# A chunk-selecting attention with a layer-norm MLP on one core: the hand-written order of all steps laid out anew, with 24 fewer products on zeros

## The chip, the core and the metric

The kernel runs on one core of a Trainium2 chip. A core has five engines that run side by side, each its own list of instructions in order: TensorE (PE: products; its weight loads are shown as PEld), VectorE (DVE), ScalarE (ACT), GpSimd (POOL) and SyncE (SP), which here only asks for transfers. Transfers (DMA) are asked for from SP, ACT and POOL. SBUF is the memory that the engines work from, PSUM the small memory that PE writes its results to. The metric is the device time of one execution in microseconds (us); the median of three runs is given.

## What is computed

Two stages, both in one kernel; shapes are batch 4, 8 heads, sequence 768, head width 64, and a model width of 512 with a hidden width of 2048.

```python
k_min, k_max = min and max of k over chunks of 32 positions      # 24 chunks
ub = sum_d max(q * k_min, q * k_max), later chunks masked         # bound of each query on each chunk
top_chunks = argsort(ub)[..., -6:]
scores = q k^T / 8, kept where the key's chunk is chosen and key <= query
x = softmax(scores) v, heads side by side                         # 4 x 768 x 512
xn = (x - mean) / sqrt(var + 1e-6) * g_ln
out = x + max(xn @ w_ch1, 0) @ w_ch2
```

## The kernel before

**Tiles and stages.** A sequence is six tiles of 128 positions. A *group* g (0 to 15) is a pair of heads of a batch: g = 4 * batch + pair. The groups of batch 0 (0 to 3) are loaded and prepared tile by tile for all heads at once (steps with a name ending in t: ldt, turnt, kboundt, and so on); the first tile of every batch has its own steps (names ending in a: lda, turna, smma, sexpa, diaga, valuesa, norma; the number is the batch); the groups 4 to 15 are prepared one by one (ldb, turn, kbound, ...). The MLP works on *units* u of two or three tiles: units 0 and 1 are the first tiles of the batches, unit 2 + 2b holds tiles 1 and 2 of batch b, unit 3 + 2b its tiles 3 to 5.

**Steps.** Each step is a small function; its parts go to one engine, or to two or three.

| what | steps | engine, lines |
|---|---|---|
| loads of q and k | ldt.tile.kn/qn, lda.batch.kn/qn, ldb.group.kn/qn | SP, the lda of q ACT; L233, L206, L216 |
| loads of v, W1 and W2 in quarters | ldvt, ldva, ldv; w1.j; w2.j | POOL; L242, L209, L226; L190; L199 |
| q and k turned, so that the head width lies on the partitions | turnt, turna; turn | PE into PSUM, L254, L355; DVE, L427 |
| k bounds of a tile | kboundt, kbounda; kbound | DVE, L259/260, L360/361; L460/461 |
| k copied into the ring of keys | kcopyt, kcopya, kcopy | ACT, L122 (a helper's line) |
| bounds laid out for the product | kdiagt, kdiag | POOL, L270 to L279; L471 to L477 |
| q high part, low part, positive parts | qhit, qlot, qrelt, qringt | ACT L288; DVE L291, L297/298, L122 |
| bound products, mask, mask turned, mask into the ring | boundst, lowst, selectt, masktt, mringt | PE L311; ACT L122; DVE L327 to L332; PE L340; DVE L122 |
| scores, exponential, causal edge | smm/smma, sexp/sexpa, diag/diaga | PE L563, L381; ACT L574, L388; POOL L582, L395 |
| times v, divided | values/valuesa, norm/norma | PE L598, L406; DVE L612, L415 |
| layer norm | pstat/pstata, centre, rstd | DVE L649, L421; L659; DVE and POOL L667, L670 |
| normalized x turned | xtp and xtc (units 0, 1, 2), xt (others) | PE L683 and ACT L122; a transposing DMA from SP, L676 |
| W1 times the gain g_ln, by quarters | w1g.j | DVE L196 |
| first and second product of the MLP | m1.unit.m, relu, m2.unit.tile.j | PE L701; ACT L717; PE L730 |
| result, store | fin | DVE L739; SP L744 |
| mask rows, constants | rows, rows0, rrows.i; ident, idh, masks, caus, small, ones | POOL L134 to L139, POOL L183/184, DVE L122; POOL and DVE |

m1.u.m needs the W1 quarter m // 4, which w1g must have scaled; m2.u.i.j needs W2's quarter j and the relus of hidden part j.

**Products on zeros.** A step written with `@n`, where it runs on PE, is preceded by n products of 128x256 on a tile of zeros, into the PSUM tile that the step is about to write (`busy`, L116). Their result is overwritten. They keep PE busy while it has nothing to do. Before the first real step `warm.14` does fourteen of them.

**What sets the order.** The string ORDER lists all 956 steps. The loop behind it calls them one after the other and chains every instruction to the one before it on the same engine, so each engine's list, and SP's, ACT's and POOL's lists of transfers, have exactly this order:

```python
for ins in done[n:]:
    if ins.engine in queues:
        if ins.engine in ahead:
            tc.add_manual_dep(ins, ahead[ins.engine], inorder, reason="order")
        ahead[ins.engine] = ins.name
```

Waits between engines are put in by the framework from what each instruction reads and writes. It also makes two engines that read the same PSUM tile do so in the order of the list: a kcopyt that stands behind the kboundt of the same tile waits for it, and the other way round.

**Buffers.** PSUM is two pools: four small tiles (ps_t: turned tiles, bounds, masks, times-v of groups, second MLP product) and two large ones (ps_m: scores, first MLP product, times-v of first tiles). Loaded q and k tiles of 128x768 or less share six buffers (ldp), so the n-th load waits for the turn of the load six before it.

Of the kernel before, what the change touches and what calls it, by code (L numbers as in the profile page):

```python
# [19 lines left out]
def kernel(  # L20
# [714 lines left out]
    def fin(u, i, e=None):  # L735
# [147 lines left out]
```

## Time and profile before

| | us |
|---|---|
| median of 3 runs (283.73 to 283.98) | 283.79 |
| the profiled execution, its own time | 283.73 |
| its span, first to last instruction | 282.0 |
| PE busy | 265.9 |
| DVE busy | 208.5 |
| ACT busy | 181.4 |
| POOL busy | 110.2 |
| bytes moved | 31.01 MB |

The profile is one execution. Its parts read here: busy tenths of each engine in 40 slices; busy time by stretch; the timeline of one engine (start, length, line, output, input, idle before and what released it); the chain of work that ended last, followed back from the end; transfers with the time from request to landing. Busy times of PE overlap a little at their ends, which are modelled, so lengths of PE work are taken from start to start.

PE's first real product starts at 4.19 us, the unbroken stretch of MLP products at 41.80 us, and the last product ends at 278.8 us; DVE has most of its work done at 205 us, after which PE still has about 75 us of products.

### The profile page before, as it was taken

To read this page: it belongs to the slowest core of one execution; us is meant where nothing else is said; L and a number is where in the kernel's file an instruction comes from. 1 tells how busy PE (TensorE), PEld (TensorE's weight loads), DVE (VectorE), ACT (ScalarE), POOL (GpSimd) and SP (SyncE) were. 2 spreads that over 40 slices of the span, in tenths; PEclk is the share of its full clock that TensorE was granted. 3 is DMA by queue.
4 is the path that set the end of the run, shared out by engine and by line. 5 is a ranking of instruction groups with operands and counts; after the bars stand their busy time and mean duration, and the time that the engine had idled before them with its cause. 6 is when DMAs were issued, how large, how long until landed. Compare 5 with 4: busy or idle time off the path is not lost.

```text
span 282.0 us, 7100 instructions
## 1 busy us (share of the span) xinstructions
PE 265.9 (94%) x2785; PEld 188.2 (67%) x2785; DVE 208.5 (74%) x604; ACT 181.4 (64%) x241; POOL 110.2 (39%) x209
## 2 busy tenths in 40 slices
PE   8775889899999999899999999989999999999995
PEld 5654779687677666666786676669666665765552
DVE  5978999936999999899999999998835162501111
ACT  2365786643799896878779778886686575222420
POOL 8883847070524407958162252645230121100000
PEclk9999999999999999999999999999999999999999
DMA  8999999999368979997595769358140102021102
GB/s 164 209 207 187 138 154 142 190 135 116 25 120 175 188 107 140 123 149 108 97 125 128 124 162 136 53 86 76 30 127 2 40 37 74 19 42 74 74 9 105
DMA packets 126897, 31.01 MB, mean 110 GB/s; under 512 B 118032, under 2 KB 123920, under 8 KB 126864
## 3 DMA queue, kind: packets, MB, share of 16 engines
q1 hardware_dynamic: 92848, 22.16, 40.5%
q0 software_dynamic: 29328, 7.34, 27.8%
q10 hardware_dynamic: 4688, 1.05, 2.5%
q8 instruction: 22, 0.36, 0.6%
q14 instruction: 11, 0.09, 0.1%
HBM read 27.27 MB, written 6.29 MB: 119 GB/s over the span
## 4 chain that ended last, share of the span: by engine, by line
PE 75%; DVE 12%; POOL 4%; ACT 3%; issue 2%; SPq 2%; DMA 1%; DVEq 0%; POOLq 0%; ACTq 0%
PE mm L701 28%; PE yp L730 25%; PE mm L563 10%; PE sm L598 5%; PE ub L484 3%; DMA knb<-in_k_dram 1%; SPq L216 1%; PE trh L514 1%; ACT KB L122 1%; DVE bst L649 1%; DVE KA L122 1%; DVE KB L122 1%; POOL bdt L273 1%; ACT KA L122 1%; DVE kcs L260 1%
## 5 line engine op out<-in xcount | busy, mean ns | idle before, releaser
L574 ACT ACTIVATE pt<-mm 128x1024 f16<-128x1024 f32 (+2 forms) x96 | 81.9, 881 | 23.5 <-PE mm L563 22.2
L730 PE MATMUL yp<-w2b,hT 128*128 128x512 f16 (+2 forms) x400 | 93.6, 370 | 0.2 <-DVE x L612 0.2
L701 PE MATMUL mm<-xT,w1b 128*128 128x256 f16 (+1 forms) x640 | 89.5, 294 | 1.4 <-ACT hT L717 1.3
L717 ACT ACTIVATE hT<-mm 128x768 f16<-128x768 f32 (+1 forms) x56 | 50.2, 901 | 42.0 <-PE mm L701 38.5
L701 PEld LDWEIGHTS <-w1b 128*128 128x128 f16 x640 | 61.5, 98 | 22.4 <-issue 2.0
L730 PEld LDWEIGHTS <-hT 128*128 128x128 f16 x400 | 37.1, 98 | 32.1 <-issue 0.4
L739 DVE SCALAR_TENSOR_TENSOR ot<-yp,rstd,x 128x512 f32<-128x512 f32 (+2 forms) x25 | 17.7, 722 | 32.1 <-PE yp L730 18.1
L582 POOL TENSOR_SCALAR_AFFINE_SELECT pt<-pt 128x512 f16<-128x512 f16 (+1 forms) x32 | 24.8, 779 | 38.1 <-ACT pt L574 38.0
L563 PE MATMUL mm<-QA,KA 128*128 128x128 f16 (+2 forms) x224 | 33.2, 242 | 1.2 <-ACT pt L574 0.9
L563 PE MATMUL mm<-QB,KB 128*128 128x128 f16 (+2 forms) x224 | 33.1, 242 | 0.0
L670 POOL TENSOR_TENSOR rstd<-ve,mhalf 128x2 f32<-128x2 f32 (+1 forms) x10 | 9.3, 937 | 51.9 <-DVE ve L667 51.9
L598 PEld LDWEIGHTS <-pt 128*128 128x128 f16 x640 | 22.9, 97 | 3.3 <-issue 0.9
L563 PEld LDWEIGHTS <-KA 128*128 128x128 f16 x224 | 17.8, 98 | 10.7 <-issue 1.5
L598 PE MATMUL sm<-va,pt 128*128 128x65 f16 x520 | 23.5, 193 | 0.8 <-DVE ot L739 0.8
L226 POOL DMA_DIRECT2D va<-in_v_dram x24 | 21.3, 887 | 1.1 <-issue 0.8
L563 PEld LDWEIGHTS <-KB 128*128 128x128 f16 x224 | 17.9, 98 | 3.6 <-issue 0.2
L611 DVE RECIPROCAL rden<-sm 128x4 f32<-128x4 f32 (+1 forms) x32 | 5.7, 178 | 17.7 <-PE sm L598 17.3
L612 DVE TENSOR_TENSOR x<-sm,rden 128x256 f32<-128x256 f32 (+1 forms) x32 | 15.7, 491 | 1.1
L649 DVE BATCH_NORM_STATS2 bst<-x 128x6 f32<-128x256 f32 x40 | 14.3, 408 | 0.1
L116 PEld LDWEIGHTS <-zer 128*128 128x128 f16 x83 | 7.9, 97 | 6.8 <-issue 5.2
L659 DVE TENSOR_SCALAR xc<-x,mv 128x512 f16<-128x512 f32 x24 | 11.8, 541 | 0.0
L471 POOL TENSOR_TENSOR kcs<-kcs 128x24 f32<-128x24 f32 x12 | 3.5, 292 | 20.0 <-DVE kcs L461 19.9
(115 smaller groups left out, 383.0 us busy)
## 6 DMA issues: line engine op xcount, KB each, us to landing
out_dram<-ot SPq DMA_DIRECT2D x23, 256.0 KB, 2.1
qnb<-in_q_dram SPq DMA_DIRECT2D x48, 80.0 KB, 3.3
knb<-in_k_dram SPq DMA_DIRECT2D x48, 80.0 KB, 3.3
w1b<-in_moe_w_ch_dram POOLq DMA_DIRECT2D x4, 512.0 KB, 8.6
w2b<-in_moe_w_ch_dram POOLq DMA_DIRECT2D x4, 512.0 KB, 7.1
va<-in_v_dram POOLq DMA_DIRECT2D x24, 80.0 KB, 4.1
knt<-in_k_dram SPq DMA_DIRECT2D x5, 256.0 KB, 7.3
qnt<-in_q_dram SPq DMA_DIRECT2D x5, 256.0 KB, 10.7
```

The costliest lines, as they stand in the source:

```text
L226: nc.gpsimd.dma_start(va[:, hh, :, 0:D], v[b, 2 * hp + hh, P:S].rearrange("(t p) d -> p t d", p=P))
L563: nc.tensor.matmul(sc[:, hh, o:o + w * P], ks[:, (t - 1) * P:t * P] if t else k0, qs[:, (s - 1) * P:(s - 1 + w) * P], start=True, stop=True,)
L574: nc.scalar.activation(st[g]["pt", r][:, 4 * i:4 * i + o].rearrange("p n h x -> p h n x"), st[g]["sc", r, i][:, :, 0:o * P].rearrange("p h ...
L582: nc.gpsimd.affine_select(out=dv, in_=dv, compare_op=ALU.is_ge, fill=0.0, base=0, pattern=[[0, 2 * (z - a)], [1, P]], channel_multiplier=-1,)
L598: nc.tensor.matmul(pv[:, hh, s - a, :], pt[:, where[t, s], hh, :], va0[:, b * H + 2 * hp + hh, 0:D + 1] if t == 0 else sb[t]["va"][:, 2 * ...
L612: nc.vector.tensor_tensor(xt_(unit(b, r))[:, :, 2 * hp:2 * hp + 2, :].rearrange("p s h d -> p h s d"), pv[:, :, :, 0:D], rden.to_broadcast ...
L649: nc.vector.bn_stats(half(u)["st"][:, i, hp // 2], flat(xt_(u)[:, i, 2 * hp - 2:2 * hp + 2]))
L659: pick(nc.vector, nc.gpsimd).tensor_scalar(h["xc"][:, i, :], flat(xt_(u)[:, i]), h["mv"][:, i, 0:1], None, op0=ALU.subtract,)
L701: nc.tensor.matmul(hp_[:, i // (per(u) // 2), o:o + w], w1b[:, kt, (m + i) * P:(m + i + 1) * P], h["xT"][:, kt], start=(kt == 0), stop=(kt ...
L717: nc.scalar.activation(o, i, ACTF.Relu, scale=HS)
L730: nc.tensor.matmul(h["yp", i][:, cs], h["hT", kt // 4][:, kt % 4, i * P:(i + 1) * P], w2b[:, kt, cs], start=(kt == 0), stop=(kt == KT2 - 1),)
L739: nc.vector.scalar_tensor_tensor(ot[:, cs], h["yp", i][:, cs], h["rstd"][:, i:i + 1], flat(xt_(u)[:, i])[:, cs], op0=ALU.mult, op1=ALU.add,)
```

## The change

ORDER has the same 956 steps before and after; only their order differs, and the numbers behind @. No function is changed. Products on zeros go from 83 to 59 (warm.14 is untouched): the last column of this table gives the steps that have them after the change.

| | before | after |
|---|---|---|
| first SP loads | k1, q2, k2, k of batch 0, q1 | q2, q1, k2, k1, k of batch 0 |
| DVE list from its start | zeros small rrows.1 rrows.0 qlot.2 kboundt.1 | zeros small masks rrows.0 idh rrows.1 rrows.2 rrows.3 qringt.2 qlot.2 |
| DVE list after mringt.1 | pstata.0 norma.1 pstata.1 kbounda.1 kbounda.3 | kboundt.3 kbounda.3 norma.1 norm.3.0 pstata.1 |
| ACT list around it | sexp.3.0.0 kcopya.3 sexp.0.0.0 | sexp.3.0.0 sexp.1.0.0 kcopya.3 sexp.0.0.0 |
| POOL list with W1 | kdiagt.2 ldvt.1 w1.0 caus diaga.0 diaga.1 diag.3.0 ldva.3 w1.1 diag.0.0 ldva.2 w1.2 ... rstd.0 w1.3 | ldva.1 diaga.0 ldvt.2 w1.0 diaga.1 diag.3.0 diag.1.0 ldva.3 diag.0.0 diag.2.0 w1.1 diaga.3 w1.2 ldva.2 w1.3 |
| PE list from m1.0.0 | m1.0.0 valuesa.3 xtp.2 smma.2 turnt.4.kn turnt.4.qn m1.2.0 m1.0.4 valuesa.2 turnt.3.qn boundst.4 m1.2.4 m1.0.8 m1.2.8 | m1.0.0 turnt.4.kn valuesa.3 xtp.2 smma.2 turnt.3.qn m1.2.0 m1.2.4 m1.0.4 m1.2.8 turnt.5.qn valuesa.2 boundst.4 turnt.5.kn m1.0.8 m1.0.12 |
| steps with products on zeros | turnt.2.kn 6, turna.0.kn 6, turnt.1.qn 12, turna.0.qn 16, turna.1.kn 2, boundst.2 11, boundst.1 3, turna.3.qn 6, smm.3.0.1 1, smm.0.0.1 6, smm.2.0.1 5, values.1.0 4, valuesa.3 2, turnt.4.qn 3 | turnt.1.qn 6, turnt.2.kn 6, turnt.1.kn 6, turna.0.kn 6, turna.1.kn 10, boundst.2 3, turna.1.qn 4, turna.3.kn 9, valuesa.1 3, values.3.0 2, smm.0.0.1 2, turnt.4.qn 2 |

The diff, cut to the beginning and the end of the string:

```diff
-        zeros warm.14 rows small ldt.1.kn ldt.2.qn ldt.2.kn ident turnt.1.kn turnt.2.qn qhit.2 lda.0.kn rows0
-        lda.0.qn turnt.2.kn@6 ldva.0 rrows.1 turna.0.kn@6 rrows.0 qlot.2 ldt.1.qn kboundt.1 kdiagt.1 kbounda.0
-        kdiagt.0 kcopyt.1 kcopyt.2 ones ldva.1 lda.1.kn rrows.3 qrelt.2 rrows.2 turnt.1.qn@12 lda.1.qn ldvt.2
-        turna.0.qn@16 kboundt.2 lda.3.qn lda.3.kn qhit.1 idh turna.1.kn@2 kcopya.0 kdiagt.2 ldvt.1 lda.2.qn
-        kcopya.1 w1.0 qringt.2 qlot.1 qcopya.0 boundst.2@11 lowst.2 caus qringt.1 qrelt.1 boundst.1@3 smma.0
-        masks turna.3.qn@6 selectt.2 masktt.2 lowst.1 selectt.1 sexpa.0 diaga.0 turna.1.qn valuesa.0 qcopya.1
-        smma.1 qcopya.3 masktt.1 mringt.2 sexpa.1 norma.0 lda.2.kn turna.3.kn smm.3.0.1@1 mringt.1 pstata.0
-        diaga.1 sexp.3.0.1 smm.1.0.1 sexp.1.0.1 smm.3.0.0 valuesa.1 norma.1 gain ldt.3.kn smm.0.0.0 sexp.3.0.0
-        pstata.1 kcopya.3 diag.3.0 ldva.3 values.3.0 ldt.4.kn smm.1.0.0 w1.1 ldt.4.qn sexp.0.0.0 diag.0.0
-        sexp.1.0.0 smm.0.0.1@6 sexp.0.0.1 ldva.2 kbounda.1 smm.2.0.1@5 values.0.0 kbounda.3 norm.3.0 smm.2.0.0
-        turna.2.qn w1.2 sexp.2.0.0 centre.0 diag.1.0 qcopya.2 norm.0.0 sexp.2.0.1 diag.2.0 values.1.0@4 xtp.0
-        w1g.0 ldt.3.qn ldt.5.kn smma.3 xtc.0 values.2.0 turnt.3.kn norm.1.0 norm.2.0 pstat.1.0 sexpa.3
-        turna.2.kn pstat.3.0 centre.2 diaga.3 kboundt.3 kcopya.2 m1.0.0 valuesa.3@2 kdiagt.3 xtp.2 relu.0.0
-        norma.3 w2.0 smma.2 kcopyt.3 turnt.4.kn turnt.4.qn@3 xtc.2 w1g.1 sexpa.2 diaga.2 kboundt.4 qhit.4 m1.2.0
-        m1.0.4 kbounda.2 relu.2.0 qlot.4 qrelt.4 valuesa.2 half_ kdiagt.4 turnt.3.qn rstd.0 norma.2 qhit.3 w1g.2
-        boundst.4 m1.2.4 lowst.4 pstata.2 relu.0.4 w1.3 selectt.4 relu.2.4 qlot.3 m1.0.8 kcopyt.4 pstata.3
-        m1.2.8 masktt.4 relu.0.8 w2.1 m2.2.0.0 turnt.5.kn m2.0.0.0 relu.2.8 centre.1 mringt.4 kboundt.5 w1g.3
-        kcopyt.5 m2.0.1.0 xtp.1 m1.2.12 rstd.1 ldt.5.qn m1.0.12 relu.2.12 xtc.1 qrelt.3 relu.0.12 ldb.4.qn
-        ldb.4.kn m2.0.0.1 w2.2 qringt.3 turnt.5.qn qringt.4 kdiagt.5 qhit.5 qlot.5 m1.1.4 boundst.3 qrelt.5
-        relu.1.4 lowst.3 selectt.3 m1.1.12 boundst.5 lowst.5 w2.3 selectt.5 m2.0.1.1 m1.1.0 masktt.5 m2.0.1.2
-        m2.0.0.2 ldb.5.qn relu.1.12 mringt.5 relu.1.0 masktt.3 turn.4.qn qringt.5 mringt.3 m1.1.8 smm.1.1.3
-        turn.4.kn ldvt.5 rstd.2 m2.2.1.0 m2.2.0.1 qhi.4 kbound.4 ldvt.4 sexp.1.1.3 smm.1.1.1 relu.1.8 qlo.4
...
-        relu.9.0 relu.9.6 m1.9.4 relu.9.4 m1.9.14 m1.9.12 fin.7.0 m2.9.0.0 relu.9.12 relu.9.14 m2.9.0.1 m2.9.2.0
-        m2.9.0.2 m2.9.0.3 m2.9.2.1 fin.9.0 m2.9.1.0 m2.9.1.1 m2.9.1.2 m2.9.1.3 fin.9.2.0 m2.9.2.2 fin.9.1
-        m2.9.2.3 fin.9.2.1
+        zeros warm.14 rows ldt.2.qn ldt.1.qn ident small ldt.2.kn rows0 ldva.0 turnt.2.qn masks rrows.0 qhit.2
+        idh turnt.1.qn@6 rrows.1 qhit.1 ones rrows.2 rrows.3 lda.0.qn ldt.1.kn lda.1.qn qringt.2 turnt.2.kn@6
+        qlot.2 lda.0.kn qlot.1 caus gain turnt.1.kn@6 lda.1.kn kboundt.2 kboundt.1 turna.0.kn@6 kbounda.0
+        kcopyt.1 ldvt.1 qringt.1 kcopya.0 qrelt.1 qrelt.2 turna.1.kn@10 kdiagt.2 turna.0.qn kdiagt.1 kdiagt.0
+        lda.2.qn kcopyt.2 kbounda.1 ldva.1 ldt.3.kn lda.3.kn qcopya.0 boundst.2@3 smma.0 lowst.2 boundst.1
+        sexpa.0 selectt.2 turna.1.qn@4 diaga.0 lda.2.kn lowst.1 kcopya.1 masktt.2 ldt.4.qn qcopya.1 smma.1
+        selectt.1 lda.3.qn turnt.3.kn mringt.2 valuesa.0 sexpa.1 norma.0 masktt.1 turna.3.kn@9 smm.1.0.1
+        kcopyt.3 smm.3.0.1 pstata.0 sexp.3.0.1 turna.2.qn ldvt.2 mringt.1 sexp.1.0.1 w1.0 smm.3.0.0 smm.1.0.0
+        qcopya.2 diaga.1 sexp.3.0.0 valuesa.1@3 sexp.1.0.0 kcopya.3 ldt.4.kn kboundt.3 diag.3.0 values.3.0@2
+        kbounda.3 norma.1 diag.1.0 norm.3.0 smm.0.0.0 values.1.0 smm.2.0.0 sexp.0.0.0 ldva.3 pstata.1 centre.0
+        smm.0.0.1@2 sexp.2.0.0 diag.0.0 diag.2.0 turna.3.qn norm.1.0 turna.2.kn smm.2.0.1 sexp.0.0.1 qcopya.3
+        w1.1 xtp.0 ldt.3.qn sexp.2.0.1 w1g.0 values.0.0 values.2.0 xtc.0 smma.3 norm.0.0 turnt.4.qn@2 sexpa.3
+        norm.2.0 kcopya.2 pstat.1.0 m1.0.0 pstat.3.0 diaga.3 w1.2 turnt.4.kn valuesa.3 ldt.5.qn qhit.4 centre.2
+        ldt.5.kn qlot.4 xtp.2 relu.0.0 ldva.2 xtc.2 norma.3 smma.2 qrelt.4 ldb.4.qn sexpa.2 turnt.3.qn w1.3
+        w1g.1 kboundt.4 qringt.4 kdiagt.3 diaga.2 w2.0 kdiagt.4 m1.2.0 ldb.5.qn w2.1 half_ w1g.2 m1.2.4 relu.2.0
+        ldb.4.kn m1.0.4 qhit.3 relu.2.4 m1.2.8 relu.0.4 ldb.7.qn turnt.5.qn rstd.0 relu.2.8 valuesa.2 qlot.3
+        boundst.4 lowst.4 kbounda.2 pstata.3 kcopyt.4 qrelt.3 turnt.5.kn m1.0.8 norma.2 w1g.3 ldvt.3 relu.0.8
+        kcopyt.5 kboundt.5 m1.0.12 qhit.5 boundst.3 m1.2.12 selectt.4 pstata.2 m2.0.0.0 rstd.2 ldb.5.kn qlot.5
+        centre.1 m2.0.1.0 kdiagt.5 lowst.3 qringt.3 xtp.1 relu.2.12 qrelt.5 m2.0.0.1 ldb.8.kn selectt.3 w2.2
+        boundst.5 turn.4.qn xtc.1 relu.0.12 m2.0.1.1 qhi.4 masktt.3 mringt.3 ldb.6.kn w2.3 m1.1.12 qringt.5
+        m1.1.0 masktt.4 lowst.5 relu.1.12 turn.5.qn selectt.5 m2.0.1.2 m2.0.0.2 masktt.5 m1.1.8 mringt.5
+        relu.1.0 mringt.4 smm.1.1.0 m2.2.0.0 qhi.5 relu.1.8 smm.1.1.1 qlo.5 sexp.1.1.0 sexp.1.1.1 turn.4.kn
+        diag.1.1 ldvt.4 m2.0.0.3 smm.1.1.3 sexp.1.1.3 ldvt.5 kbound.4 m2.0.1.3 smm.0.1.0 m1.1.4 sexp.0.1.0
+        smm.0.1.1 relu.1.4 qlo.4 rstd.1 sexp.0.1.1 qrel.4 turn.5.kn m2.2.0.1 kdiag.4 smm.0.1.3 bounds.4
+        sexp.0.1.3 diag.0.1 lows.4 smm.0.1.2 m2.2.0.2 qring.4 qrel.5 kbound.5 smm.1.1.2 sexp.0.1.2 m2.2.0.3
+        ldb.8.qn smm.3.1.3 kdiag.5 kcopy.4 select.4 fin.2.0 sexp.1.1.2 values.0.1 sexp.3.1.3 m2.2.1.0 smm.3.1.1
+        ldb.6.qn smm.3.1.0 turn.7.qn fin.0.1 ldb.11.qn values.1.1 ldb.7.kn qhi.7 norm.0.1 sexp.3.1.1 qlo.7
...
+        m2.8.1.3 m1.9.0 relu.9.2 fin.7.2 relu.9.0 fin.8.1 fin.7.0 m1.9.12 m1.9.4 relu.9.12 m1.9.6 relu.9.4
+        relu.9.6 m1.9.10 m1.9.14 m2.9.1.0 m2.9.0.0 relu.9.14 relu.9.10 rstd.9 m2.9.1.1 m2.9.1.2 m2.9.1.3
+        m2.9.2.0 fin.9.1 m2.9.2.1 m2.9.0.1 m2.9.0.2 fin.9.2.0 m2.9.0.3 m2.9.2.2 fin.9.0 m2.9.2.3 fin.9.2.1
```

## The prediction

> **What bounds the kernel now.** First the page's slices (tenths busy, 7.05 us each), then busy time by stretch, the waits, the chain and single engines' timelines. The slices:
>
> ```profile
> PE   8775889899999999899999999989999999999995
> DVE  5978999936999999899999999998835162501111
> ```
>
> TensorE (PE) has holes up to 42 us and hardly any after; VectorE (DVE) is nearly full from 14 to 200 us. Columns by stretch: length, then busy us of PE, PEld, DVE, ACT, POOL, clock, DMA share, GB/s:
>
> ```profile
> 0.00:10.00 10.00, 8.46 (x56) 6.37 (x57) 6.91 (x12) 2.15 (x3) 8.01 (x13) 1.00 1.02 180
> 10.00:20.00 10.00, 7.03 (x89) 5.70 (x88) 8.60 (x22) 6.14 (x13) 9.44 (x30) 1.00 1.51 207
> 20.00:30.00 10.00, 6.20 (x88) 5.00 (x86) 9.01 (x34) 6.43 (x10) 4.41 (x6) 1.00 1.45 192
> ...
> 57.00:100.00 43.00, 42.99 (x484) 31.30 (x482) 35.26 (x108) 32.41 (x42) 16.30 (x33) 1.00 0.83 126
> 100.00:120.00 20.00, 18.71 (x196) 12.47 (x195) 18.71 (x52) 15.62 (x23) 12.60 (x24) 1.00 0.94 124
> 120.00:262.00 142.00, 141.05 (x1507) 97.27 (x1505) 100.17 (x298) 95.81 (x123) 46.22 (x80) 1.00 0.51 84
> ```
>
> So PE's work after 57 us costs its own length; idle there is 0.01 + 1.29 + 0.95 = 2.25 us. The end is set by when PE's unbroken stretch starts and by those 2.25 us. What releases that start, in the chain (start, length, what):
>
> ```profile
> 38.84 0.68 DVE kcs L260
> ...
> 39.57 0.56 issue
> 40.14 0.58 ACT KB L122
> 40.74 1.02 ACT xT L122
> 41.80 3.65 PE mm L701 x32
> ...
> 54.39 0.61 DVE kcs L260
> 55.08 0.58 ACT KA L122
> 55.67 0.59 ACT KB L122
> 56.30 0.61 PE xq L683 x8
> ```
>
> VectorE's in-order list reaches kboundt.3 (L259/260), ScalarE's kcopyt.3 (L122) waits for it, xtc.2 stands behind, and m1.2.0 begins at 41.80. At 55 us it recurs with tile 5: PE waits 0.91 us before xtp.1. VectorE from 3.35 us:
>
> ```profile
> 3.35 0.32 DVE L122 COPY KA<-RT 64x640 f16<-64x640 f16 x1 [2.04 <-POOL RT L139]
> 3.68 0.32 DVE L122 COPY KB<-RT 64x640 f16<-64x640 f16 x1
> 4.02 1.94 DVE L122 COPY KA<-RT 64x640 f16<-64x640 f16 x1
> ```
>
> The same copy takes 0.32 or 1.94 us; the long one lies under POOL's rows0 copies (1.88 us each).
>
> ```profile
> w1b<-in_moe_w_ch_dram POOLq DMA_DIRECT2D x4, 512.0 KB, 8.6
> ```
>
> One by one the W1 quarters took 11.1, 8.0, 9.3 and 7.0 us to land.
>
> [...] PE's ramp gaps are at most 1.2 us here and the clock reads 1.00 in every stretch.[...]
>
> **The change part by part.** Step durations below come from the trace (us): kbound of a tile 1.2, qlot 0.6, qrelt 0.85, qringt 0.6, selectt 1.4 to 1.6, mringt 0.86, norma 0.92, pstata 0.6, norm 0.55, pstat 0.65, centre 1.1 to 1.2, w1g 1.15 to 1.5 on VectorE; kcopy 1.18, sexp and relu 0.93, xtc 1.0 on ScalarE; m1 1.75, m2 0.87, a turn 0.47 on PE. I walk the new lists with these.
>
> *Products on zeros.* 24 of 83 go. Each costs 0.109 us (twelve from 8.55 to 9.86 us): 2.6 us, but they stand where PE waits anyway. Bounds: 0 to -2.6 us; I take 0, cover being the ramp's VectorE chain.[...] the new gaps I find are below 2 us, so 0.
>
> *VectorE up to mringt.1.* The masks (1.0 us, once at 17.5) move into the 2.04 us idle before the RT rows; two of four rrows still fall beside rows0. rrows end near 9.4; qringt.2, qlot.2, qlot.1 to 11.3; kboundt.2, kboundt.1, kbounda.0 to 14.9. K tile 0 is now SP's fifth load; the first five landed at 4.0, 5.2, 6.4, 7.7 and 8.9 us, so loads are early. kcopyt.1, kcopya.0, kcopyt.2 end at 17.3 on ScalarE, which frees the PSUM buffer of turna.0.qn; boundst.2 waits for three kdiags on POOL (1.55 to 2.5 us each) to about 18.2; selectt.2 starts at 19.05. Its mask constant, behind ldvt.1 and w1.0 in POOL's list before (0.96 us lost at 20.2), now comes early. mringt.1 ends near 25.7, before 26.2, with kbounda.1 and pstata.0 done in addition. Uncertainty 1 us each way: the three kdiags.
>
> *A new wait.* VectorE now has kboundt.3 and kbounda.3 straight after mringt.1. kbounda.3 must wait for ScalarE's kcopya.3, which stands behind sexp.3.0.0 and sexp.1.0.0, which need mringt.1: 0.6 + 0.93 + 0.93 + 1.18 = 3.7 us after mringt.1, while kboundt.3 fills 1.2. VectorE idles 2.6 us; queued behind: norma.1, norm.3.0, pstata.1, centre.0, w1g.0, hence xtp.0 and m1.0.0. That eats the lead: w1g.0 ends at 36.0 (34.8 before). Gained back: kboundt.3 and kcopyt.3 no longer stand before xtc.2. centre.2 39.6, xtp.2, xtc.2, m1.2.0 at 41.45 against 41.80: **-0.35 us**.
>
> *W1 and the queues.* w1.0 now stands behind diaga.0 and ldvt.2: asked for at 22.1, at 11.1 us landed by 33.3, wanted 34.5. w1.1 waits for diag.2.0: 32.3, lands 40.3 to 41.6, wanted 41.9. w1.2 stands behind diaga.3 (sexpa.3 ends 36.6): asked for at 37.8. At 7.0 us it lands at 44.8, wanted at 44.95; at 9.3, 47.1. DMA moved 154 GB/s around 35 to 42 us, below the 207 of the ramp, so I take 7.0: cost 0, range 0 to 3.7 us (11.1 us). w1.3 and W2 land before use. Beside w1.3, ldva.2 and diaga.2 move on POOL; SP's reordered loads only run further ahead (the worst, ldb.9.kn, gets some 13 us).
>
> *Around xtp.1.* w1g.3 ends near 52.1, just as m1.0.8 does. kboundt.5 now waits for kcopyt.5, behind relu.0.8: 2.1 us idle on VectorE, then 5.3 us to centre.1: 59.6. PE has m1.0.12, boundst.3, m1.2.12, two m2 = 5.8 us: it waits 1.75 us at xtp.1 (0.91 before). Comparing equal PE work at the m2.0.0.1 after it (after 61.1, lacking one m2 and one mask turn, ahead by boundst.3: 61.65 against 61.7): **-0.05 us**.
>
> *57 us to the end.* Same work on every engine. I summed step lengths along both lists. Leaving idle out, PE's least lead over VectorE is 1.6 us in the new order (smm.1.1.0 waiting for mringt.4), then 3.5 (bounds.6) and 3.7 (smm.7.1.1); before 5.9, 6.3, 6.6. But VectorE idled 4.4 us at 58 us before and, less PE's own gaps, about 2 to 3 in the new order; both end near zero. Before, 1.29 us went at 105 to 114 because ScalarE's kcopy.7 waited for turn.7.kn (SP fetched k of group 7 only at 91 to 95 us); the new SP list asks for it some 18 us of VectorE work ahead. Bounds for the new idle: 0 to 4.5 us (twice the old); I take half of 2.25: **-1.1 us**. The last steps (small m2.9.2.3, fin.9.2.1, store) are unchanged, 3.2 us after the last product.
>
> **Sum.** The profiled execution took 283.73 us, 282.0 of span and 1.73 around it; the median is 283.79. 283.73 - 0.05 - 1.1 = 282.6, and 0.1 for the many small waits that a walk misses: **282.7 us**.
>
> **Rivals.**
> (a) *The W1 request comes too late: slower.* w1.2 lands late, m1.2.8 on PE (due 46.7) waits for w1g.2, everything behind it, w1g.3 and xtp.1 too. PE's wait is landing + 1.5 - 46.7: with 9.3 us 1.9, with 11.1 3.7. From 8.5 us on it outweighs the gain. For: 8.0, 9.3 and 11.1 seen, and w1.3 follows on the same queue. Against: 7.0 and W2's 5.8. With 0.3 us for leads lost later: 282.7 + 1.9 + 0.3 = 284.9.
> (b) *The middle only trades its stalls*, 2.25 us as before: 283.7, no change. For: leads equally thin. Against: the late load is gone.
> (c) *The removed zeros were in the way*: -2.6 instead of the ramp's -0.05, with the middle as before: 281.1. For: PE reads 8.46 busy in the first 10 us. Against: the chain there runs through VectorE.
> (d) The change not doing what it says is excluded: the built program has 24 products fewer and the new order on every engine.
>
> **Chances.** Forecast 0.38, own range 281.9 to 283.2; (a) 0.36; (b) 0.20; (c) 0.06. Faster by over 0.2% (0.57 us, about what this kernel's measurement can tell from no change) is the forecast with (c): 0.44; same 0.20; slower 0.36. Range: low 281.4, which leaves out most of (c); high 286.0, most of (a)'s 3.7 us: 282.7 + 3.3.
>
> **What would show it.** mringt.1 ending at 25 to 26.5; a VectorE gap near 2.6 us before kbounda.3 (L360); m1.2.0 at 41 to 42; w1.2 landing 7 us after its request and no PE wait before m1.2.8; 1.5 to 2 us of PE wait at xtp.1; PE idle after 62 us near 1 us. Wrong if PE's unbroken stretch starts after 43, or PE waits more than 2 us between 62 and 262 us.

## The result and the profile after

The changed kernel is slower: 287.65 us median of 4 runs (286.66 to 287.98) against 283.88 us for the kernel before (283.73 to 285.24), ratio 1.0116 (of the averages; that of the medians is 1.0133), 95% interval 1.0076 to 1.0156. The forecast was 282.7, its range ended at 286.0. The profiled execution took 286.66 us, 284.9 of it span, 2.9 more than before.

The page's slices after (tenths busy, now 7.12 us each; PEclk is TensorE's granted clock):

```profile
PE   8667789979999979999999999999999999999995
...
DVE  7988799696989996799999998999955272402212
...
PEclk9899999999999997999999999999999999999999
```

Counted from 1, TensorE's row of nines now has a hole at slice 15 (99.7 to 106.8 us), and VectorE (DVE) has one at 16 and 17, just behind it. (The seven at slice 9 is the wait at xtp.1.) PEclk was 9 throughout before; it drops in slices 2 and 16.

Busy time by stretch after (length; busy us of PE, PEld, DVE, ACT, POOL; clock, DMA share, GB/s):

```profile
10.00:20.00 10.00, 6.75 (x70) 5.32 (x70) 9.13 (x18) 4.58 (x9) 6.52 (x23) 0.83 1.59 198
...
57.00:100.00 43.00, 41.03 (x451) 28.49 (x449) 38.71 (x124) 31.74 (x40) 14.37 (x30) 1.00 0.76 122
100.00:120.00 20.00, 18.00 (x150) 10.94 (x149) 16.21 (x37) 13.39 (x20) 12.51 (x24) 0.91 1.31 142
120.00:262.00 142.00, 141.73 (x1542) 98.40 (x1541) 104.49 (x311) 97.01 (x125) 47.08 (x80) 1.00 0.49 81
...
107.20:110.62 3.42, 3.42 (x13) 1.66 (x11) 1.61 (x3) 1.65 (x3) 0.54 (x1) 0.50 1.52 148
```

The last line shows what a row of nines hides: from 107.20 to 110.62 us TensorE is busy all the time, but at half its clock: m1.3's products start 0.32 us apart there and 0.163 us apart afterwards, so half of 3.42 us, 1.7 us, is lost while "busy". So the 2.9 us are made up like this: TensorE idles 2.5 us more (18.6 against 16.1 in the whole span: +1.1 before 42 us, -0.6 from there to 57, +2.0 from 57 to 100, +0.7 from 100 to 120, -0.7 from 120 to 262), zeros take 2.6 us less (24 x 0.109), and half clock adds about 3.0 (by difference, since busy time rises by 0.4 in spite of the zeros: 1.7 here, the rest near 12 us). The 2.0 us before 100 us are mostly the wait at xtp.1, which before fell ahead of 57 us, and a wait for W2. This sum fills the span; which part of it delays the end is what the experiments ask.

The two gaps that precede the two drops, in TensorE's timeline after:

```profile
7.83 0.62 PE L254 MATMUL tr<-ident_f,knt 128*128 128x128 f32 x4
11.27 1.13 PE L116 MATMUL tr<-zer 128*128 128x256 f16 x6 [2.82 <-DVE q L291]
...
13.04 2.24 PE L116 MATMUL tr<-zer 128*128 128x256 f16 x10
...
103.73 0.39 PE L563 MATMUL mm<-QB,KB 128*128 128x128 f16 x4
106.11 8.18 PE L701 MATMUL mm<-xT,w1b 128*128 128x384 f16 x39 [2.00 <-DMA xT<-xc]
```

At 8.45 us the next step in TensorE's list is turna.0.kn, whose zeros, too, wait for a PSUM buffer that qlot.2 on VectorE frees; at 104.11 m1.3.8 waits for xT of unit 3. The ten zeros at 13.04 start 0.21 us apart instead of 0.109.

The chain of waits after (start, length, what) around the second gap:

```profile
96.53 0.88 DVE xc L659 x2
...
100.65 0.55 SPq L676
...
101.25 4.73 DMA xT<-xc
...
106.11 7.05 PE mm L701 x32
```

centre.3 (L659) ends at 97.4 us; the last of the three transposing DMAs (xt.3.1) starts only at 101.25 and takes 4.7 us, where the fastest of the three took 2.7. Meanwhile POOL loads v of groups 5 and 4 (its timeline after):

```profile
100.37 1.81 POOL L226 DMA_DIRECT2D va<-in_v_dram  x2
...
102.22 1.73 POOL L226 DMA_DIRECT2D va<-in_v_dram  x2
```

Before, the transposing DMAs were asked for at 96.9 to 99.5 us, v of group 4 at 93.9 to 95.7 and v of group 5 after 109. SP's timeline and the tile xT between 92 and 112 us, before:

```profile
96.86 4.42 SPq L676 DMA_TRANSPOSE xT<-xc  x3
...
DMA to landing us min/median/max: 3.0/3.6/4.5
```

and after:

```profile
98.60 3.90 SPq L676 DMA_TRANSPOSE xT<-xc  x3
...
DMA to landing us min/median/max: 2.7/3.1/4.7
```

The last of the three was asked for at 99.52 us and took 3.0 before; after, it is asked for at 101.25 and takes 4.7. So it lands 3.4 us later, half of it by the place in SP's list and half by the landing.

What was foretold for the start is there: VectorE's wait before kbounda.3 (L360), in its timeline after,

```profile
30.40 0.69 DVE L360 TENSOR_REDUCE kcs<-tr 128x16 f32<-128x512 f32 x1 [2.30 <-ACT KB L122]
```

and W1 in time: of the tile w1b after, the wait of TensorE's products for the rescaled quarters (0.3 us, once) and the transfers.

```profile
  PE mm L701: 0.3, 1
...
DMA to landing us min/median/max: 5.3/8.0/10.9
```

### The profile page after: what moved, and what is told of

It is laid out like the page before. It is cut to its first block, busy times and chain, and to the rows that moved or that the text cites. A ratio compares the mean times of both kernels' runs of the same rounds, so it can differ in the third digit from the quotient of the medians.

```text
span 284.9 us, 7056 instructions
## 1 busy us (share of the span) xinstructions
PE 266.3 (93%) x2761; PEld 187.2 (66%) x2761; DVE 211.8 (74%) x604; ACT 182.0 (64%) x241; POOL 109.8 (39%) x209
## 4 chain that ended last, share of the span: by engine, by line
PE 60%; DVE 23%; DMA 7%; POOL 4%; issue 3%; ACT 2%; SPq 0%; DVEq 0%; POOLq 0%
PE mm L701 23%; PE yp L730 20%; PE mm L563 8%; PE sm L598 5%; DMA xT<-xc 3%; DMA w2b<-in_moe_w_ch_dram 2%; PE ub L484 2%; DVE xc L659 2%; DVE bst L649 2%; DVE KB L122 1%; DVE kcs L461 1%; DVE x L612 1%; DVE KA L122 1%; DVE QB L122 1%; DVE w1b L196 1%
## 5 line engine op out<-in xcount | busy, mean ns | idle before, releaser
L701 PE MATMUL mm<-xT,w1b 128*128 128x256 f16 (+1 forms) x640 | 90.7, 297 | 2.6 <-DMA xT<-xc 2.0
L670 POOL TENSOR_TENSOR rstd<-ve,mhalf 128x2 f32<-128x2 f32 (+1 forms) x10 | 8.0, 795 | 51.4 <-DVE ve L667 51.2
L437 ACT ACTIVATE q<-qnT 128x640 f16<-128x640 f32 x12 | 8.8, 733 | 4.8 <-DMA QB<-q 3.3
L471 POOL TENSOR_TENSOR kcs<-kcs 128x24 f32<-128x24 f32 x12 | 4.3, 361 | 19.3 <-DVE kcs L461 16.0
L659 DVE TENSOR_SCALAR xc<-x,mv 128x512 f16<-128x512 f32 x24 | 11.6, 530 | 0.0
```

Of the source, the lines that this page charges most:

```text
L659: pick(nc.vector, nc.gpsimd).tensor_scalar(h["xc"][:, i, :], flat(xt_(u)[:, i]), h["mv"][:, i, 0:1], None, op0=ALU.subtract,)
L701: nc.tensor.matmul(hp_[:, i // (per(u) // 2), o:o + w], w1b[:, kt, (m + i) * P:(m + i + 1) * P], h["xT"][:, kt], start=(kt == 0), stop=(kt ...
```

## The experiments

Theory T1: the late transposing DMAs of unit 3 cost a wait and then a half clock. R1: the start is the cause. T2: the missing zeros are, by way of the clock. T4: VectorE's new wait is. Each kernel ran in several rounds beside the kernel before, and the ratios are to the kernel before in the same batch, whose median moved between 283.8 and 284.3 us. The changed kernel ran in the first batch alone, so "below the changed kernel" compares medians of two batches (287.65 us there); single traces are set beside them.

**Zeros in the gap of the middle.**

```diff
-qhi.8 m1.3.8 relu.3.8
+qhi.8 m1.3.8@18 relu.3.8
```

> The changed kernel with 18 more products on zeros (18 x 0.109 = 1.96 us) ahead of m1.3.8, in the 2.0 us in which TensorE waits for xT of unit 3. Theory T1 (the transposing DMAs of unit 3 come late: 2.0 us of wait, and then the clock is halved for 3.4 us, which costs some 1.7 us of products): the wait stays, the clock stays up, the 48 products of m1.3 take 7.8 instead of 9.6 us, the time falls by 1.7 to about 286 us. Rival R1 (the excess comes from the ramp, and this stretch is bound by VectorE and ScalarE anyway, which wait for QB at 108 us): no change, 287.6 us. If the zeros themselves are in the way: slower by up to 2 us.

Measured: 285.96 us (285.57 to 286.42), ratio 1.0075 (1.0063 to 1.0087), 1.7 us below the changed kernel, whose fastest run took 286.66. TensorE's timeline of this kernel:

```profile
104.21 2.13 PE L116 MATMUL mm<-zer 128*128 128x256 f16 x18
107.02 6.17 PE L701 MATMUL mm<-xT,w1b 128*128 128x384 f16 x37 [0.68 <-DMA xT<-xc]
```

m1.3.8 starts 0.9 us later than in the changed kernel's profile, and 8 us later the same products start 0.8 us earlier than there, because all go at full clock (1.00 from 104 to 122 us): 1.7 us between the two, in one stretch. T1's share for the clock stands, and R1 falls: this stretch is not in another engine's shadow.

**The transposing DMAs ahead of a load on SP.**

```diff
-smm.2.1.2 ldb.9.qn diag.2.1
+smm.2.1.2 diag.2.1
-smm.4.1.3 xt.3.1 turn.8.qn
+smm.4.1.3 xt.3.1 ldb.9.qn turn.8.qn
```

> The changed kernel with the load of q of group 9 (issued on SP from 96.25 to 98.5 us) moved behind the three transposing DMAs of unit 3, which are asked for right after centre.3 (97.4 us). T1 with the cause in SP's queue: they are asked for 1.1 us earlier, TensorE waits 0.9 instead of 2.0 us, and with a gap that short the clock is not halved: 1.1 + 1.7 = 2.8 us less, 284.8 us. T1 with the cause in DMA traffic or in SP's own waits between the three (1.8 us): wait nearly as before, 287.2 us or more. R1 (the ramp): no change.

Measured: 290.4 us (289.15 to 290.99), ratio 1.0227 (1.0207 to 1.0246): 2.8 us slower instead of faster. The wait for xT did go (asked for at 96.9, landed in 2.4 to 2.5 us, m1.3.8 at 104.2). Another took its place, in ScalarE's (ACT) timeline of this kernel and in TensorE's waits:

```profile
110.10 0.74 ACT L437 ACTIVATE q<-qnT 128x640 f16<-128x640 f32 x1 [4.70 <-DMA QB<-q]
```

```profile
PE mm L701 <- ACT hT L717: 4.7, 1, 4.7
```

The load, moved back, now stands ahead of qring.6 on SP; qhi.8 overwrites the q rows that qring.6 copies, so ScalarE waits for that DMA; relu.3.8 stands behind qhi.8, and TensorE runs out of PSUM buffers. In the changed kernel the same wait was there (3.28 us, until 108.46), hidden under TensorE's own. No theory had it.

**Zeros in the gap of the start.**

```diff
-gain turnt.1.kn@6 lda.1.kn
+gain turnt.1.kn@30 lda.1.kn
```

> The changed kernel with 24 more products on zeros (2.6 us) ahead of turnt.1.kn, which fill TensorE's gap of 2.82 us at 8.45 us. Theory T2 (the gap halves the clock from 11.6 to 15.1 us, and this delays the ramp): K tile transposes at full clock again, mringt.1 and m1.2.0 some 0.5 us earlier, 287.1 us. T1 or R3 (the halved clock lies in VectorE's shadow: TensorE waits again at 16.7 and 18.4 us): full clock in the trace, no change of the time within 0.2 us.

Measured: 286.55 us (285.26 to 287.8), ratio 1.0095 (1.0069 to 1.0122); its interval overlaps that of the changed kernel, so the time is inconclusive. The traces are sharper, as the same product can be found in both: the transposes at 12 to 16 us start up to 1.2 us earlier, and from 34 to 68 us every product starts 0.10 to 0.12 us later than in the changed kernel. This run had a half clock of its own, at 20.1 to 23.5 us (mean clock 0.92 from 20 to 42 us), so it alone doesn't show that the gap of 2.82 us and the half clock after it delay nothing. The splice with zeros back in its start, below, has none and does.

**v loads away from the transposing DMAs.**

```diff
-qrel.6 ldv.5 ldv.4 smm.4.1.3 ... m2.2.1.3 diag.4.0 sexp.4.0.1
+qrel.6 smm.4.1.3 ... m2.2.1.3 diag.4.0 ldv.4 ldv.5 sexp.4.0.1
```

> The changed kernel with the POOL loads of v of groups 4 and 5 (issued 100.4 to 103.9 us) moved behind diag.4.0, so that none of them is asked for before 104 us. T1 with contention as the cause of the slow landing (4.7 us for the last transposing DMA against 2.7 for the fastest): the last lands about 1 us earlier, wait 1.0 us, perhaps no halved clock: 1.0 to 2.7 us less, 285 to 286.6. T1 with the place in SP's queue as cause, or R1: no change, 287.6 us.

Measured: 284.5 us (283.45 to 287.58, 22 runs), ratio 1.0024 (1.0006 to 1.0041), 3.1 us below the changed kernel. TensorE's and ScalarE's timelines of this kernel:

```profile
103.59 2.76 PE L701 MATMUL mm<-xT,w1b 128*128 128x384 f16 x16
107.47 5.36 PE L701 MATMUL mm<-xT,w1b 128*128 128x384 f16 x32 [1.11 <-ACT hT L717]
```

```profile
105.98 0.74 ACT L437 ACTIVATE q<-qnT 128x640 f16<-128x640 f32 x1 [1.16 <-DMA QB<-q]
```

The three transfers land in 2.4 to 2.7 us (before this edit the last took 4.7), the wait for xT is gone, and of the 3.28 us wait behind qhi.8 1.16 are left. The tile xT of this kernel, 92 to 112 us:

```profile
DMA to landing us min/median/max: 2.4/2.5/2.7
```

In the profile the products after this stretch start 2.9 us earlier than in the changed kernel, 2.6 of it won between 102 and 112 us and 0.35 at 68 us, where a wait for W2 is missing. T1 with contention explains the greater part of the loss.

**Three repairs together.** Later v loads, zeros back in the start, and the relus ahead of qhi.8:

```diff
-gain turnt.1.kn@6 ... boundst.2@3
+gain turnt.1.kn@30 ... boundst.2@12
-qring.6 qhi.8 m1.3.8 relu.3.8 qlo.8 m1.3.2 m1.3.0 relu.3.2 relu.3.0
+qring.6 m1.3.8 relu.3.8 m1.3.2 m1.3.0 relu.3.2 qhi.8 qlo.8 relu.3.0
```

> The changed kernel with three repairs: the loads of v of groups 4 and 5 behind diag.4.0 (as in the run with the later v loads), 24 products on zeros more before turnt.1.kn and 9 more before boundst.2, and qhi.8 and qlo.8 behind relu.3.2 on ScalarE and VectorE (with later v loads alone, ScalarE waits 1.16 us there for the DMA of group 6's q rows, relu.3.8 stands behind it, and TensorE waits 1.1 us for a PSUM buffer). Theory T1 (this stretch holds the loss: transposing DMAs delayed by v loads, and the relus behind qhi.8): TensorE's wait at m1.3 falls below 0.3 us, 283.4 us, level with the kernel before (283.8) or just better. Rival (the relus were not what held: the wait only moves on to VectorE, whose qlo.8 and kbound.7 now come later): 284.5 us as with the later v loads alone, with the wait at a mask or group-7 step.

Measured: 283.8 us (282.9 to 285.02) against 284.3, ratio 0.9992 (0.9975 to 1.0009): level with the kernel before. Busy by stretch of this kernel:

```profile
104.00:120.00 16.00, 15.99 (x160) 10.57 (x159) 14.11 (x45) 14.21 (x20) 10.74 (x21) 1.00 1.31 159
```

TensorE idles 0.01 us there, against 1.28 us in the kernel before: the new middle does remove the old stalls, once its own waits are mended. What each of the three repairs adds was not measured one by one.

**Splices.** The first keeps the new list's first 325 steps (to 92 us) and then the rest in the old order; the second the reverse; the third starts old up to centre.3 (97 us) and goes on with the repaired new rest.

```diff
 mring.4 smm.2.1.0 lows.5 sexp.2.1.0
-values.3.1 turn.6.kn smm.2.1.2 ldb.9.qn ...
+m2.2.1.1 m2.2.1.2 table pstat.1.1 m2.2.1.3 ...
```

> A splice: the new list's first 325 steps (to about 92 us: the whole start, the W1 requests, the fewer zeros), then all other steps in the old order. Theory T1 (start costs little, the middle costs the rest): the start's lag of 0.5 us at 62 us and 0.6 us of waits up to 70 us against the old middle: 283.8 + 0.5 to 1.1 = 284.3 to 284.9. As predicted blind (start -0.05): 283.8. Rival R1 (the whole excess of 3.8 us comes from the start, the late waits being its consequence): 287 us.

Measured: 285.16 us (284.77 to 285.71) against 284.3, ratio 1.0029 (1.0015 to 1.0043). The new start costs 0.8 us, so by difference, if the two parts simply add, the new rest as changed costs about 3 of the 3.8.

```diff
 lows.5 m2.2.1.3 diag.3.1 smm.2.1.2
-smm.2.1.3 ... (the old rest)
+ldb.6.kn ldb.11.qn ldb.7.kn qhi.7 ... (the new rest)
```

> The reverse splice: the old list's first 325 steps (to about 92 us), then all other steps in the new order, with v of groups 4 and 5 loaded beside the transposing DMAs of unit 3. Theory T1: the 2.0 us wait for xT and, where the gap falls so, the halved clock after it stay: 286 to 287.3 us. Rival R1 (the start is the cause): 283 us, since the stalls of the old middle (1.29 us) are gone too.

Measured: 288.56 us (288.3 to 289.15), ratio 1.0158 (1.0134 to 1.0182), and inconclusive on T1: TensorE's waits in this kernel from 90 to 106 us are all of the making of the seam (the place where the two lists meet), none for xT. The two longest:

```profile
PE yp L730 <- DVE QB L122: 1.7, 1, 1.7
PE sm L598 <- DVE x L612: 1.5, 1, 1.5
```

```diff
 qlo.7 ldb.7.kn turn.6.kn sexp.4.1.1 kcopy.5
+xt.3.0 sexp.4.1.2 maskt.5 kbound.6 ... qring.6 ldb.9.qn ldb.11.qn ... (the repaired new rest)
```

> A splice at centre.3 (97 us): the steps that the new order does up to there, in the old order, then the rest of the new order with the later v loads and the relus ahead of qhi.8, and q of groups 9 and 11 loaded behind qring.6. If the new order loses in its start (1.2 to 1.7 us) and gains in its rest once that is repaired (1.3 us of the old stall at 104 to 116 us): 282.3 us, faster than both. Rival (the gain of the rest exists only because the engines arrive there in the new order's state, and the seam brings waits of its own, as the first old-start splice did at 92 us): 284 us or more.

Measured: 288.23 us (286.75 to 289.66), ratio 1.0141 (1.0108 to 1.0174). TensorE waits 2.5 us for ScalarE's exponentials up to 106 us and 2.3 us once more later; xT of unit 3 is in time. The rival holds: at this seam the new rest's gain doesn't come with the old start. That it is tied to the state in which the new start hands over VectorE and ScalarE fits these waits, but isn't shown: another seam was not tried.

**Fewer zeros in the old order.** Products on zeros in front of the steps of the old list, 59 instead of 83; fewer in all, and some moved to other steps. Only the steps whose number changes are shown, without those between, and not all of them:

```diff
-turnt.1.qn@12 turna.0.qn@16 turna.1.kn@2  boundst.2@11 boundst.1@3 turna.3.qn@6 turna.1.qn   valuesa.1
+turnt.1.qn@6  turna.0.qn    turna.1.kn@10 boundst.2@3  boundst.1   turna.3.qn   turna.1.qn@4 valuesa.1@3
-turnt.1.kn   turna.3.kn   values.3.0   smm.3.0.1@1 smm.0.0.1@6 smm.2.0.1@5 values.1.0@4 valuesa.3@2 turnt.4.qn@3
+turnt.1.kn@6 turna.3.kn@9 values.3.0@2 smm.3.0.1   smm.0.0.1@2 smm.2.0.1   values.1.0   valuesa.3   turnt.4.qn@2
```

> The kernel before, in its own order, with the new numbers of products on zeros before each step (59 instead of 83: among others none before turna.0.qn in place of 16, 3 before boundst.2 in place of 11). As predicted blind (zeros cost nothing, they stand where TensorE waits anyway): 283.8 us, no change. Rival (c) (the zeros were in the way): up to 2.6 us less, 281.2. Rival (their absence lets the clock be halved in the start): a window of 3.4 us at half clock in the trace; with VectorE holding the start no change, else up to 1 us more.

Measured: 285.68 us (284.95 to 287.48) against 284.3, ratio 1.0057 (1.0033 to 1.0082). "Cost nothing" falls, and rival (c) has the wrong sign. Every run had a lowered clock (mean 0.982 to 0.994; by estimate one to three times 3.41 us at half clock, each of which takes 3.41 / 2 in 283 us, 0.006, off the mean); the profiled one ran at half clock from 13.2 to 20.0 us (mean 0.83 in the first 20 us). Its products start 0.52 us later than before's from 42 to 103 us (VectorE waits 1.08 instead of 0.31 us for valuesa.1, which now stands behind zeros), and 1.36 us later from 112 us on, after a wait of 1.1 us for xT, whose DMAs landed after up to 4.1 us. So not all of the 1.6 us (0.57% of the time) is the clock.

**More zeros in the old order.**

```diff
-turna.0.qn@16 ... turna.3.qn@6
+turna.0.qn@26 ... turna.3.qn@14
```

> The kernel before with 18 more products on zeros in its start: 26 instead of 16 ahead of turna.0.qn, 14 instead of 6 ahead of turna.3.qn, where TensorE then waits 1.2 us. In the profiles of the old order in which the clock was halved at 24 or at 16 and 30 us, the start is 1.2 to 1.4 us late. Theory T2' (in the old order such a halving[...] makes the difference between runs of 283.7 and of 285.2 us): fewer runs near 285.2, median 283.7, mean clock of more runs 1.00. Rival (these zeros delay steps that VectorE or ScalarE wait for): 284 to 285 us in all runs.

Measured: 283.68 us (283.64 to 285.14), ratio 0.9993 (0.9978 to 1.0008): 13 of 14 runs at a mean clock of 1.00, all between 283.64 and 284.08, and one at 0.993 with 285.14. The kernel before, beside it: 25 of 43 runs at 1.00 (median 283.68), 15 at 0.994 (median 284.31), 3 at 0.987 (median 285.27), which by that estimate is 3.41 us at half clock once and twice. So the clock was up in more of the runs with more zeros. The time itself is the same within the interval; that the 83 zeros earned their time in this way is likely from the clock and the run times, but not shown, since the run with fewer zeros lost time in other ways too.

**VectorE's new wait**, in the repaired order and in the splice of new start and old rest:

```diff
-kbounda.3 norma.1 diag.1.0
+norma.1 kbounda.3 diag.1.0
```

> The repaired new order (v loads later, zeros put back, relus ahead of qhi.8: 283.8 us) with kbounda.3 moved behind norma.1 on VectorE, so that the 2.3 us for which VectorE waits for kcopya.3 are partly filled. In the trace the repaired order is some 1.7 us behind the kernel before at 92 us for the same products done. Theory T4 (this new wait makes the start late): w1g.0, m1.0.0 and all that follows up to 0.9 us earlier, 283.0 us. Rival (the start is late for other reasons: POOL's bounds, W2's landing at 68 us, the waits at xtp.1): within 0.3 us of 283.8.

> The splice of the new start with the old rest (285.16 us, its runs within 284.8 to 285.7) with kbounda.3 behind norma.1 on VectorE. Theory T4 (VectorE's new wait for kcopya.3, 2.3 us in the trace, makes the start late by 0.9 us): 284.3 us. Rival (the wait is absorbed before 92 us and the start is late because the clock is halved in it or because of W2): 285.0 to 285.4, no change.

Measured: 283.53 us (282.24 to 285.38) against 283.81, ratio 0.9977 (0.9957 to 0.9996), the only kernel here that beats the one before, and just; and for the splice 284.14 us (283.7 to 285.15) against 283.78, ratio 1.0007 (0.9994 to 1.0021), where it had 1.0029. VectorE's timeline of the repaired order with this edit:

```profile
29.20 0.21 DVE L414 RECIPROCAL rdena<-mm 128x8 f32<-128x8 f32 x1 [1.12 <-PE mm L406]
29.44 0.69 DVE L415 TENSOR_TENSOR x<-mm,rdena 128x512 f32<-128x512 f32 x1
30.38 0.69 DVE L360 TENSOR_REDUCE kcs<-tr 128x16 f32<-128x512 f32 x1 [0.24 <-ACT KB L122]
```

norma.1 fits into the wait, and in the repaired order each product from 34 to 112 us starts 0.85 to 0.93 us earlier than in the profile without the edit; in the splice 0.5 us earlier from 42 to 68 us, though that run had half clock from 16.6 to 23.4 us (mean clock 0.92 in the first 20 us and 0.92 from there to 42). (From 68 us on it is 1.0, but the other half is a wait for W2 that this profile lacks.) The medians say less for the repaired order: 283.53 lies within 0.3 us of 283.8, which was the rival's sign. For the splice they agree with T4: 284.14 instead of 285.16. So T4 stands, for 0.5 to 0.9 us by the traces, and with this one wait shortened the new start is level with the old within the interval.

**Zeros back in the new start**, same splice:

```diff
-turnt.1.kn@6 ... boundst.2@3
+turnt.1.kn@30 ... boundst.2@12
```

> The same splice of new start and old rest, with 24 more products on zeros ahead of turnt.1.kn and 9 more ahead of boundst.2, so that the clock is not halved at 11 to 15 us. Rival T2 (fewer zeros, hence the halved clock, make the new start late): 0.5 us or more less, 284.6 or lower. T4: no change, 285.0 to 285.4, at a granted clock of 1.00 instead of 0.988 to 0.994.

Measured: 284.57 us (284.46 to 285.07, 22 runs), ratio 1.0017 (1.0006 to 1.0028), nearly all at a clock of 1.00. The time is down by about 0.3 (by the ratios) to 0.6 (by the medians), as T2 wanted, yet not where T2 puts it: in the traces both kernels' products start at the same times (within 0.02 us) from 20 to 68 us, though the splice ran at half clock from 11.1 to 14.5 us (mean clock 0.91 in the first 20 us) and this kernel didn't (1.00): that half clock delayed nothing. The 0.44 us between them from there to the end are a wait for W2's landing that this profile lacks. The kernel with later v loads has the changed kernel's list up to 97 us and lacks that wait too, so it comes and goes without an edit; whether more zeros make it rarer stays open.

**k of group 7 first, in the old order.**

```diff
-ldb.8.kn ... ldb.7.kn
+ldb.7.kn ... ldb.8.kn
```

> The kernel before with one exchange on SP: k of group 7 is asked for where k of group 8 was, and k of group 8 where k of group 7 was. As said in the prediction, the 1.29 us of TensorE idle at 104 to 116 us come from turn.7.kn and kcopy.7 being late because k of group 7 was loaded late: 1 us less, 282.8 us. Rival (k of group 7 is not what ends that wait; ScalarE's relus behind kcopy.7 are late because of the transposes on VectorE, not of the load): no change, 283.8 to 284.3 us, or a wait for turn.8.kn in its place.

Measured: 283.76 us (283.68 to 285.25), ratio 1.0003 (0.9986 to 1.002): nothing. TensorE's two waits of the old middle, in its timeline of this kernel:

```profile
108.05 2.76 PE L701 MATMUL mm<-xT,w1b 128*128 128x384 f16 x16 [0.28 <-ACT hT L717]
...
116.34 0.97 PE L701 MATMUL mm<-xT,w1b 128*128 128x384 f16 x5 [1.00 <-ACT hT L717]
```

They are as in the kernel before, whose two lines are

```profile
106.61 2.76 PE L701 MATMUL mm<-xT,w1b 128*128 128x384 f16 x16 [0.28 <-ACT hT L717]
...
114.89 1.46 PE L701 MATMUL mm<-xT,w1b 128*128 128x384 f16 x8 [1.00 <-ACT hT L717]
```

The load wasn't what made the relus late.

**v loads put beside the transposing DMAs, in the old order.**

```diff
-turn.6.qn ldv.4 m2.1.1.1 ... diag.4.1 ... qring.6 ldv.5 qrel.7
+turn.6.qn m2.1.1.1 ... diag.4.1 ldv.4 ldv.5 ... qring.6 qrel.7
```

> The kernel before with the loads of v of groups 4 and 5 both right behind diag.4.1 on POOL, so that they are asked for at 96.5 to 100 us, beside the three transposing DMAs of unit 3 (97 to 101 us). T1 (v loads beside them delay the transposing DMAs): TensorE waits for xT ahead of m1.3.2 by 1 to 2 us, in some runs followed by a halved clock: 285 to 287 us. Rival (the old order has slack there, or the delay in the new order came from something else that moved with it): no change, 283.8 to 284.3 us.

Measured: 286.78 us (285.49 to 290.64), ratio 1.0091 (1.0059 to 1.0123, without the run of 290.64). The two runs at a mean clock of 1.00 took 285.49 and 286.09, about 2 us more than the kernel before at that clock. TensorE's timeline and the tile xT in this kernel:

```profile
107.59 5.36 PE L701 MATMUL mm<-xT,w1b 128*128 128x384 f16 x32 [2.02 <-DMA xT<-xc]
```

```profile
DMA to landing us min/median/max: 6.1/6.4/6.9
```

With only the place of these two loads changed, the transfers last 6.1 to 6.9 us (3.0 to 4.5 before) and the wait for xT appears. (The profile also has half clock at 24.3 us, mean clock 0.92 from 20 to 42 us, and its products at 98 us start 1.2 us late.) T1's mechanism is shown from both sides: with these loads moved away in the changed kernel the slowest of the three took 2.7 instead of 4.7 us, with them put beside here 6.9 instead of 4.5.

## Why the prediction was wrong, step by step

*Products on zeros: "so 0", since "the new gaps I find are below 2 us".* Wrong twice. There are gaps of 2.82 us (8.45 us) and 2.00 us (104.11 us); the walk has VectorE's low parts of q end at 11.3 us and doesn't ask what TensorE does until they free its buffer. And that gaps below 2 us leave the clock up was the author's estimate, not shown by a trace: the profile before has none above 1.20 us ahead of its last product. In the profile after, 3.41 us at half clock come behind each of the two gaps, from 11.62 and from 107.20 us; in the 3.41 us before the second (103.79 to 107.20 us) TensorE was busy for 1.41 us, 41%. The bound of the term should have been 1.7 us, half of 3.41, for each, with a chance for it. What it cost: 1.7 in the middle (shown; no zeros were taken away there, the gap is that of the late transposing DMA), in the old order up to 1.6 for fewer zeros, of which part came by other ways; in the new start nothing that the traces show before 68 us, with an open 0.4 us after that.

*VectorE to mringt.1: 25.7.* It ended at 26.9: selectt.2 began at 19.67 (19.05 in the walk), held by ScalarE's ubl copy, and its last operation (L332) took 1.07 us (0.92 in the profile before).

*A new wait: 2.6 us, w1g.0 at 36.0, m1.2.0 at 41.45, -0.35.* The mechanism was right (2.30 us, w1g.0 ends at 36.4) and the sum too small: m1.2.0 began at 41.89. "That eats the lead" was said, and then taken as paid back by centre.2's earlier turn. Moving kbounda.3 behind norma.1 shows that it still cost 0.5 to 0.9 us in the traces.

*W1: 0.* Right. The quarters were asked for at 22.8, 33.9, 38.4 and 40.1 us (22.1, 32.3 and 37.8 predicted for the first three) and m1.2.8 didn't wait. Rival (a), with 0.36 the likeliest loss, did not happen. This was close, and in part luck: w1.2 took the 7.0 us that were assumed, its rescaling ended at 47.5 us, and m1.2.8 began at 47.8; the four quarters took 9.1, 5.3, 7.0 and 10.9 us.

*Around xtp.1: net -0.05.* The wait was 1.37 us (1.75 predicted), m2.0.0.1 ended at 61.70 instead of 61.1, so the start was 0.55 us behind by the prediction's own comparison. A wait for W2 of 0.4 us at 68 us, which I had excluded, came on top; the splice puts the new start at +0.8 us.

*57 us to the end: -1.1.* This is the step that failed most, and by sign. I summed step lengths along the lists for VectorE's lead over TensorE and treated SP's and POOL's moves as loads that "only run further ahead". The lead that mattered was that of a transfer. From the end of centre.3 to m1.3.8 TensorE has 6.7 us of work. The transposing DMAs stand 1.2 us behind a q load, the third is asked for 2.7 us after the first, and it takes 4.7 us to land beside two v loads that the new POOL list puts there: 8.6 us. Instead of -1.1 the stretch from 97 to 116 us gave 2.0 of wait and 1.7 of half clock, less the 1.28 us of old stalls; from 120 to 262 us 0.7 was gained (0.27 idle instead of 0.95), more than half as foretold. That is +1.7 in sum; with the 0.55 of the start and the 0.4 for W2 it makes 2.7 of the profile's 2.9 us. The old stalls did vanish with the new order, but the cause that I gave for them, the load of k of group 7, was wrong (and its reading too: SP asked for it at 93.6 to 96.0 us, not at 91 to 95).

*The rivals.* None named a half clock or xT; that the time came out slower, as rival (a) had it, is no merit of its cause. Of the two signs by which the text said it would be wrong, one came: TensorE waited 2.7 us between 62 and 262 us (more than 2), while its unbroken stretch started at 41.9 (not after 43).

What stays open: why runs of the repaired order with kbounda.3 moved spread from 282.2 to 285.4 us at a mean clock of 1.00, where those of the old order with more zeros lie within 0.44 us; and how much of the changed kernel's 3.8 us falls to the wait and how much to the clock in each run, since the mean clock of its four runs went from 0.981 to 0.988.

## What to carry to other kernels

When an order is laid out anew, walk the transfers with the steps: for each DMA that a matmul needs, the time from its producer to its last issue, plus landing beside what other queues have in flight then, against TensorE's work in between. Look for coupling through one in-order list: a copy that waits for a DMA (qhi.8) in front of relus that TensorE needs turns one late transfer into the next wait, as moving one load showed. And price every new TensorE idle time of about 2 us (2.00 us was followed by half clock in the changed kernel, 2.02 us in the old order with v loads beside was not) at up to 1.7 us, half of the 3.41 us that one half clock lasted, on top of its length, or fill it with products on zeros that nothing waits for.

## What the runs showed of the hardware

The clock. In the profile after, TensorE's clock is halved twice ahead of its last product, both times for 3.41 us: from 11.62 us, behind a wait of 2.82 us, and from 107.20 us, behind one of 2.00 us. In the 3.41 us ahead of each TensorE was busy for 0.60 and 1.41 us. The profile before, whose longest wait is 1.20 us, stays at 1.00 up to 262 us. The length of the wait alone doesn't tell: behind one of 2.46 us (until 12.62 us) the old order with fewer zeros ran at half clock for 6.8 us, and the stretch of the 4.7 us wait in the kernel with the transposing DMAs ahead reads 0.86 (104 to 116 us), but waits of 3.0 us in the kernel with zeros in the gap of the start, of 2.02 us in the old order with v loads beside (both in a 104 to 116 us that reads 1.00) and of 2.3 us in the splice with the repaired rest (106 to 262 us, 1.00 in each part) had no half clock behind them. What makes the difference was not shown. The levels of one kernel go with it: 3.41 us at half clock lower the mean clock of a run by 0.006 (3.41 / 2 in 283 us), and the medians of the kernel before in the last batch were 283.68, 284.31 and 285.27 us at mean clocks of 1.00, 0.994 and 0.987. Over all 127 of its runs they are 283.71, 284.31 and 285.20, but single runs at 0.994 lie anywhere from 283.05 to 285.34.

What a half clock cost differed with the engine that the end waits for there: 1.7 us for 3.41 us where TensorE is the bound (the changed kernel against the one with zeros before m1.3.8); nothing in the new start (11.1 to 14.5 us in the splice; in the profile after TensorE waits again, 0.54 us until 16.71 and 1.17 us until 18.37); and in the old order's start it goes with a delay: its profile with k of group 7 first, half clock at 16.6 and at 30.3 us (mean clock 0.92 in the first 20 us and 0.92 from there to 42), is 1.45 us late from 42 us on, and the one with v loads beside, half clock at 24.3 us (0.92 from 20 to 42), 1.21.

The repeatability. Apart from such events the same product starts at the same time to within 0.02 us from 20 to 68 us in the two splices that share a list there, with and without zeros (TensorE busy 18.14 and 18.16 us from 42 to 62 us). So one event that differs, like W2's landing at 68 us, can be read from two single profiles, where medians of five rounds only show that something did.
